# Chunk 0 in two halves with chunk 1's convolutions between, a moved weight load, and a reordered backward tail, in a speech joint-network kernel

## The chip, the core and the metric

The kernel runs on one core of a Trainium2 chip, in one launch that computes the forward pass and all gradients. The metric is the device time in microseconds (us). PE is the matmul engine, DVE the vector engine, ACT the scalar engine, POOL is GpSimd, and SP issues most of the loads.

## What is computed

```python
# x (2,16000,256), w1, w2 (3,256,256), g (2,8,256), w_f, w_g, w_o (256,256), bfloat16
h = gelu(conv(x, w1))[:, ::2]          # 3 taps, every second row kept
f = gelu(conv(h, w2))[:, ::2]          # again: (2,4000,256)
j = tanh((f @ w_f)[:, :, None] + (g @ w_g)[:, None])   # (2,4000,8,256)
out = j @ w_o
# returned: out, and by jax.vjp of grad_out (2,4000,8,256) the gradients of
# x, w1, w2, g, w_f, w_g, w_o
```

gelu is the tanh approximation; the kernel writes it as x times a sigmoid.

## The kernel before

The 4000 rows of f of each batch are cut into 8 chunks of 512 (the last has 416), 16 chunks in all. A prologue makes chunk 0's f. Then comes one stage for each chunk n. Its main line is the joint network of chunk n, two of the eight rows of g at a time (joint_units, L602): per row u, gj (L518) squares the tanh (JSQ, L523), multiplies the loaded gradient GOT by w_o (L529, into PSUM) and lets DVE make NGZ (L531); POOL sums the NGZ over u (L550); o_block (L618) makes the output (L623, evicted by ACT, L625); gwo (L664) accumulates the gradient of w_o. weave (L681) threads a second line, fill, between the units of the main line. It holds the backward pass of chunk n-1 and the convolutions of chunk n+1, in the order of the list parts (L775):

- conv_units (L227): first convolution of chunk n+1, an even and an odd half ("par"), 12 matmuls each (L246); ACT evicts (L249); the gelu follows (L197), and its derivative (L199)
- d1_units (L324, matmul L336) and d5_units (L345, matmul L366): gradient back to GF, then to GH (DVE, L369)
- gwf_units (L384, products L406) and gw2_units (L413, products L437): gradients of w_f and w_2. Their operands are first turned into rows by PE transposes (L380) and copied from PSUM (L382)
- conv2_units (L264, matmul L279), fe_units (L293, matmul L302): chunk n+1's second convolution, its gelu (FT), and FE, which the tanh (L312) reads
- e_units (L443): GH is transposed into rows in two units (L462), then per block the gradient of x (gx_block, L465, matmul L478, evicted at L481, stored at L490) and in between the gradient of w_1 (gw1, L494, matmul L500)

gelu returns its operations in two lists. The first (square, scale, sigmoid, product) is queued in later, the second (the derivative) in lazy; pump (L194) issues them a few at a time, lazy ones when later is empty. flush (L318) adds a product in PSUM to the accumulators ACC1, ACC2, ACCF.

The code's order is not yet the order on the engines: a scheduler reorders the instructions at build time, each engine then runs its own list strictly in order, and keep_in_program_order pins an instruction. All PSUM tiles but one share a ring of 7 buffers (psp, L98), taken in turn, so the eighth tile waits until the first was read. JSQ has a ring of two (jsp, L92), so the JSQ for a row u must wait for the NGZ that read the JSQ two rows earlier.

In the prologue (L692 to L760) chunk 0 goes through the same functions with its gelu split by halves of the channels (HALVES, L225), the nine blocks of the weights are transposed for the backward pass (transposed_units, L730, copied by DVE at L743), and warm (L707) issues matmuls on zeros whose result nobody reads. In the stage of chunk 0, jr_block (L597) transposes the tanh on PE; later a DMA does it. At the end (L813 on) the backward pass of chunk 15 runs alone, then the accumulators are rounded and stored, and the small gradients of g and w_g follow.

Of the kernel before, what the change touches and what calls it, by code (L numbers as in the profile page):

```python
# [22 lines left out]
P = 128  # L23
# [9 lines left out]
def kernel(  # L33
# [96 lines left out]
    def load_x(n, c):  # L130
        b, ci, c0, W = geom(n)
        t = xcp.tile([P, KT, CW + 16], BF16, name="XC")
        if c == 3 and ci > 0:
            nc.sync.dma_start_transpose(out=t[:, :, 0:W + 16], in_=xq[b, c, c0 - 16:c0 + W, :])
        else:
            if c == 3:
                nc.vector.memset(t[:, :, 0:16], 0.0)
            nc.sync.dma_start_transpose(out=t[:, :, 16:16 + W], in_=xq[b, c, c0:c0 + W, :])
        S[n]["X", c] = t
# [61 lines left out]
    def gelu(xb, W, h, gp, off, kts=((0, KT),), spare=False):  # L201
# [3 lines left out]
        first, second = [], []  # L205
        for (k0, k1) in kts:
            sq_, s_, x_ = sq[:, k0:k1, :W], s[:, k0:k1, :W], xb[:, k0:k1, :W]
            h_, gp_ = h[:, k0:k1, off:off + W], gp[:, k0:k1, off:off + W]
            first += [
                partial(nc.scalar.activation, out=sq_, in_=x_, func=ACT.Square, scale=ROOT_K),  # L210
                partial(STT, out=s_, in0=sq_, scalar=1.0, in1=x_, op0=ALU.add, op1=ALU.mult),
                partial(nc.scalar.activation, out=s_, in_=s_, func=ACT.Sigmoid, scale=GELU_A),
                partial(TT, out=h_, in0=s_, in1=x_, op=ALU.mult),
            ]
            second += [
                partial(TS, out=sq_, in0=sq_, scalar1=3.0 * GELU_A, scalar2=GELU_A, op0=ALU.mult, op1=ALU.add),
                partial(TS, out=gp_, in0=s_, scalar1=-1.0, scalar2=1.0, op0=ALU.mult, op1=ALU.add),
                partial(TT, out=sq_, in0=sq_, in1=gp_, op=ALU.mult),
                partial(TT, out=sq_, in0=sq_, in1=h_, op=ALU.mult),
                partial(TT, out=gp_, in0=sq_, in1=s_, op=ALU.add),  # L220
            ]
        return first, second


    HALVES = ((0, 1), (1, 2))  # L225

    def conv_units(n):  # L227
        b, ci, c0, W = geom(n)
        seconds = []
        st = S[n]  # L230
        HT = htp.tile([P, 2, KT, CW + 2], BF16, name="HT")
        G1 = g1p.tile([P, 2, KT, CW + 2], BF16, name="G1")
        st["HT"], st["G1"] = HT, G1
# [4 lines left out]
        taps = {0: ((1, 0, 0), (2, 1, 0), (0, 3, -1)), 1: ((0, 1, 0), (2, 3, 0), (1, 2, 0))}  # L238
        for par in range(2):
            xb = gel.tile([P, KT, CW], BF16, name="g_x")  # L240
            for mt in range(KT):
                ps = ps_f32()
                k = 0
                for (i, c, sh) in taps[par]:
                    for kt in range(KT):
                        nc.tensor.matmul(ps[:, :W], lhsT=W1[:, i, kt, mt * P:(mt + 1) * P],  # L246
                                         rhs=st["X", c][:, kt, 16 + sh:16 + sh + W], start=(k == 0), stop=(k == 5))
                        k += 1
                nc.scalar.copy(out=xb[:, mt, :W], in_=ps[:, :W])  # L249
                yield  # L250
            first, second = gelu(xb, W, HT[:, par], G1[:, par], 2, HALVES if n == 0 else ((0, KT),), n == 0)
            later.extend(first)
            seconds += second
            if n == 0:
                pump(len(first))
        lazy.extend(seconds)
        if ci > 0:
            lazy.append(lambda: nc.gpsimd.tensor_copy(out=G1[:, :, :, 1:2], in_=S[n - 1]["G1h"][:]))
        if ci < NCH - 1:
            st["G1h"] = halo.tile([P, 2, KT, 1], BF16, name="G1h")  # L260
            lazy.append(
                lambda: nc.gpsimd.tensor_copy(out=st["G1h"][:], in_=G1[:, :, :, CW + 1:CW + 2]))

    def conv2_units(n):  # L264
        b, ci, c0, W = geom(n)
        st = S[n]
        HT = st["HT"]
        if n > 0:
            pump(len(later))
        FT = ftp.tile([P, KT, CW], BF16, name="FT")  # L270
        G2 = ftp.tile([P, KT, CW], BF16, name="G2")
        st["FT"], st["G2"] = FT, G2
        xb = gel.tile([P, KT, CW], BF16, name="g_x")
        for mt in range(KT):
            ps = ps_f32()
            k = 0
            for (i, par, off) in ((1, 0, 2), (0, 1, 1), (2, 1, 2)):
                for kt in range(KT):
                    nc.tensor.matmul(ps[:, :W], lhsT=W2[:, i, kt, mt * P:(mt + 1) * P],  # L279
                                     rhs=HT[:, par, kt, off:off + W], start=(k == 0), stop=(k == 5))  # L280
                    k += 1
            nc.scalar.copy(out=xb[:, mt, :W], in_=ps[:, :W])
            yield
        first, second = gelu(xb, W, FT, G2, 0, HALVES if n == 0 else ((0, KT),), n == 0)
        if n == 0:
            for f in first:
                f()
        else:
            later.extend(first)
# [3 lines left out]
    def fe_units(n):  # L293
        b, ci, c0, W = geom(n)
        if n > 0:
            pump(len(later))
# [19 lines left out]
    first_flush = {"1": True, "2": True, "F": True}  # L316

    def flush(key, acc, ps):  # L318
        if first_flush[key]:
            nc.vector.tensor_copy(out=acc, in_=ps)  # L320
        else:
            nc.vector.tensor_tensor(out=acc, in0=acc, in1=ps, op=ALU.add)  # L322

# [60 lines left out]
    def gwf_units(n):  # L384
# [24 lines left out]
        flush("F", ACCF[:], ps[:])  # L409
        first_flush["F"] = False  # L410
        yield

    def gw2_units(n):  # L413
# [19 lines left out]
        for i, place in ((1, 0), (2, 2), (0, 4)):  # L433
# [6 lines left out]
            flush("2", ACC2[:, i, :], ps[:])  # L440
            yield
        first_flush["2"] = False
    def e_units(n):  # L443
# [50 lines left out]
        def gw1(i):  # L494
# [10 lines left out]
            flush("1", ACC1[:, i, :], ps[:])  # L505

        for k, (o, M) in enumerate(bl):
# [4 lines left out]
        first_flush["1"] = False  # L512
# [184 lines left out]
    nc.gpsimd.dma_start(out=WG[:], in_=w_g.rearrange("(kt p) n -> p kt n", p=P))  # L697
    nc.sync.dma_start(out=W2[:], in_=w2.rearrange("i (kt p) n -> p i kt n", p=P))
    nc.sync.dma_start(out=WF[:], in_=w_f.rearrange("(kt p) n -> p kt n", p=P))
    nc.sync.dma_start(out=WO[:], in_=w_o.rearrange("(kt p) n -> p kt n", p=P))  # L700
    idle = xcp.tile([P, KT, CW + 16], BF16, name="XC")
    nc.vector.memset(idle[:], 0.0)
# [51 lines left out]
    for c in (1, 0, 3, 2):  # L754
        load_x(1, c)
    for _ in chain(warm(16), small_units(), conv_units(0), transposed_units(), warm(4), conv2_units(0), warm(16), fe_units(0)):
        pass
# [4 lines left out]
    for n in range(G):  # L762
        back, fwd = n > 0, n + 1 < G
        conv = conv_units(n + 1) if fwd else iter(())
        parts = []
        if back:
            for (o, M) in blocks(window(n - 1)[1] - window(n - 1)[0]):
# [7 lines left out]
                      islice(d5, 1), islice(gw2, 1), d5, islice(gw2, nhg - 2), gwf, gw2]  # L775
        else:
            parts += [conv, iter([None] * 3)]
        if fwd:
            parts.append(conv2_units(n + 1))
        if back:  # L780
            parts.append(islice(e, 6))
        else:
            parts.append(iter([None] * 3))
# [6 lines left out]
        for up in range(U // 2):  # L790
# [17 lines left out]
            if up == U // 2 - 1:  # L808
# [3 lines left out]
                lazy_on[0] = False  # L812
    n = G - 1  # L813
# [3 lines left out]
    for _ in chain(d1_units(n), d5_units(n), gwf_units(n), gw2_units(n), e_units(n)):  # L817
        pass


    for i in range(KK):
        t_ = gel3.tile([P, 512], BF16, name="g_sq", tag="g_sq")
        nc.scalar.copy(out=t_[:], in_=ACC1[:, i, :])
        nc.sync.dma_start(out=out_2[i].rearrange("(dt p) n -> p dt n", p=P), in_=t_[:].rearrange("p (k n) -> p k n", k=KT))
        t_ = gel3.tile([P, 512], BF16, name="g_s", tag="g_s")
        nc.vector.tensor_copy(out=t_[:], in_=ACC2[:, i, :])
        nc.sync.dma_start(out=out_3[i].rearrange("(dt p) n -> p dt n", p=P), in_=t_[:].rearrange("p (k n) -> p k n", k=KT))
    t_ = gel.tile([P, 512], BF16, name="g_x", tag="g_x")
    nc.vector.tensor_scalar(out=t_[:], in0=ACCF[:], scalar1=-1.0, scalar2=None, op0=ALU.mult)
    nc.sync.dma_start(out=out_5.rearrange("(dt p) n -> p dt n", p=P), in_=t_[:].rearrange("p (k n) -> p k n", k=KT))  # L830
    t_ = gel.tile([P, 512], BF16, name="g_x", tag="g_x")
    nc.scalar.copy(out=t_[:], in_=GWO_ps[:].rearrange("p k v -> p (k v)"))
    nc.sync.dma_start(out=out_7.rearrange("(dt p) n -> p dt n", p=P), in_=t_[:].rearrange("p (k n) -> p k n", k=KT))

    NGGE = const.tile([P, B, KT, U], FP32, name="NGGE")
    nc.vector.tensor_reduce(out=NGGE[:].rearrange("p b k u -> p (b k u)"),
                            in_=NGGEc[:].rearrange("p b k u c -> p (b k u) c"),
                            axis=mybir.AxisListType.X, op=ALU.add)
    NGGEb = const.tile([P, B, KT, U], BF16, name="NGGEb")
    nc.vector.tensor_copy(out=NGGEb[:], in_=NGGE[:])  # L840
    GWG_ps = ps_f32()
    for b in range(B):
        gg = ps_f32()
        for kt in range(KT):
            nc.tensor.matmul(gg[:U, 0:D], lhsT=NGGEb[:, b, kt, :], rhs=WGT[:, kt, :], start=(kt == 0), stop=(kt == KT - 1))
        gg_sb = gxp.tile([U, D], BF16, name="gg_sb")
        nc.scalar.activation(out=gg_sb[:], in_=gg[:U, 0:D], func=ACT.Copy, scale=-1.0)
# [43 lines left out]
```

## Time and profile before

| what | us |
|---|---|
| median of 3 runs | 867.71 (865.87 to 876.6) |
| the profiled execution: time | 865.23 |
| its span, first to last instruction | 863.5 |
| PE busy | 830.8 (96%) |
| ACT busy | 685.7 (79%) |
| DVE busy | 603.8 (70%) |
| POOL busy | 410.6 (48%) |
| longest chain: share of PE, DVE, ACT | 51%, 30%, 13% |

The span is 1.73 us shorter than the time of the same execution. In the profile's lines a time is a start within the span, the number after it the duration, and square brackets give the idle time before an instruction and what ended it. Instructions of an engine overlap a little: a DVE operation shown with 0.68 us lets the next one start after 0.61.

### The profile page before, as it was taken

What the parts mean: (1) busy time and instruction counts of PE and PEld (TensorE: products, weight loads), DVE (VectorE), ACT (ScalarE), POOL (GpSimd) and SP (SyncE); (2) the same over time, 40 slices, a digit from 0 to 9 for tenths busy, and PEclk for the clock granted to TensorE, in tenths of its full rate; (3) what the DMA queues carried; (4) which work ended last, traced back from release to release, by engine and by line L of the source; (5) the groups of instructions that cost most, each with busy time, mean ns of one, the idle gap of its engine ahead of it and who ended that gap; (6) DMA issues with size and microseconds to landing.
All of it is one profiled execution on the core that took longest, in us unless ns stands there. A gap on an engine that the chain in (4) does not pass through costs nothing.

```text
span 863.5 us, 17775 instructions
## 1 busy us (share of the span) xinstructions
PE 830.8 (96%) x6648; PEld 598.9 (69%) x6648; DVE 603.8 (70%) x1194; ACT 685.7 (79%) x1067; POOL 410.6 (48%) x457
## 2 busy tenths in 40 slices
PE   8878999999999999999999999999999999999997
PEld 4455776767777677777766677776766867777875
DVE  4797949669495784949578495875949579495553
ACT  4889896986969869696996969788696986969534
POOL 1264553544544544555454455453554544455651
PEclk9999999999999999999999999999999999999999
DMA  9998999999999999999899999999999999999942
GB/s 187 211 215 195 189 250 224 224 243 193 258 206 227 226 217 233 212 227 219 211 203 214 234 215 240 227 210 250 177 263 236 205 211 219 219 243 219 215 140 91
DMA packets 382455, 185.66 MB, mean 215 GB/s; under 512 B 330160, under 2 KB 366280, under 8 KB 382368
## 3 DMA queue, kind: packets, MB, share of 16 engines
q1 hardware_dynamic: 362400, 114.35, 76.4%
q0 software_dynamic: 19968, 70.18, 27.9%
q8 instruction: 52, 0.85, 0.4%
q14 instruction: 35, 0.29, 0.1%
HBM read 54.43 MB, written 50.34 MB: 121 GB/s over the span
## 4 chain that ended last, share of the span: by engine, by line
PE 51%; DVE 30%; ACT 13%; issue 3%; DMA 2%; POOL 0%; ACTq 0%; POOLq 0%; DVEq 0%
PE ps L500 7%; PE ps L246 7%; PE GWO_ps L672 7%; PE ps L529 7%; PE ps L478 7%; PE ps L623 6%; DVE NGZ L531 6%; DVE G L199 5%; DVE g_sq L199 5%; DVE g_s L197 5%; DVE GH L369 3%; ACT JSQ L523 3%; ACT JT L312 3%; PE pst L380 3%; PE ps L366 3%
## 5 line engine op out<-in xcount | busy, mean ns | idle before, releaser
L550 POOL TENSOR_TENSOR ACCN<-ACCN,NGZ 128x1024 f32<-128x1024 f32 (+1 forms) x80 | 170.4, 2130 | 126.5 <-DVE NGZ L531 124.0
L531 DVE SCALAR_TENSOR_TENSOR NGZ<-JSQ,ps 128x512 bf16<-128x512 bf16 (+1 forms) x256 | 163.4, 669 | 83.5 <-ACT GX L481 47.7
L523 ACT ACTIVATE JSQ<-JT 128x1024 bf16<-128x1024 bf16 (+1 forms) x128 | 135.3, 1060 | 86.6 <-DVE NGZ L531 86.6
L312 ACT ACTIVATE JT<-FE,GE 128x512 bf16<-128x512 f32 (+1 forms) x256 | 171.0, 736 | 0.1
L625 ACT CAST OUT<-ps 128x512 bf16<-128x512 f32 x248 | 147.7, 614 | 3.8 <-PE ps L623 3.3
L623 PE MATMUL ps<-WO,JT 128*128 128x256 bf16 x992 | 148.1, 272 | 0.9 <-DVE NGZ L531 0.5
L529 PE MATMUL ps<-GOT,WOT 128*128 128x512 bf16 (+1 forms) x512 | 138.4, 374 | 1.7 <-DVE JR L382 1.1
L672 PE MATMUL GWO_ps<-GO,JR 128*128 128x256 bf16 x992 | 139.7, 273 | 0.0
L197 DVE SCALAR_TENSOR_TENSOR g_s<-g_sq,g_x 128x1024 bf16<-128x1024 bf16 (+1 forms) x45 | 74.6, 1657 | 57.1 <-ACT g_sq L197 57.1
L623 PEld LDWEIGHTS <-JT 128*128 128x128 bf16 x992 | 94.4, 98 | 24.9 <-issue 1.4
L672 PEld LDWEIGHTS <-JR 128*128 128x128 bf16 x992 | 95.1, 98 | 18.2 <-issue 1.1
L322 DVE TENSOR_TENSOR ACC<-ACC,ps 128x512 f32<-128x512 f32 x90 | 59.4, 682 | 66.6 <-PE ps L500 62.0
L478 PE MATMUL ps<-W1T,GH 128*128 128x256 bf16 (+2 forms) x768 | 104.2, 273 | 0.0
L500 PE MATMUL ps<-rows,X 128*128 128x256 bf16 (+2 forms) x768 | 94.2, 272 | 8.2 <-DVE rows L382 8.2
L246 PE MATMUL ps<-XC,W 128*128 128x512 bf16 (+1 forms) x384 | 91.1, 374 | 2.5 <-DMA XC<-in_x_dram 2.1
L500 PEld LDWEIGHTS <-X 128*128 128x128 bf16 (+2 forms) x768 | 74.5, 98 | 23.1 <-issue 11.5
L652 POOL DMA_DIRECT2D out_dram<-OUT x64 | 49.6, 775 | 85.2 <-ACT OUT L625 82.8
L481 ACT CAST GX<-ps 128x512 bf16<-128x512 f32 (+2 forms) x128 | 74.4, 592 | 15.0 <-PE ps L478 7.8
L478 PEld LDWEIGHTS <-GH 128*128 128x128 bf16 (+2 forms) x768 | 75.0, 99 | 15.6 <-issue 1.7
L529 PEld LDWEIGHTS <-WOT 128*128 128x128 bf16 x512 | 49.1, 98 | 43.9 <-issue 2.6
L490 POOL DMA_DIRECT2D out_dram<-GX x64 | 35.9, 560 | 87.3 <-ACT GX L481 81.0
L382 ACT COPY rows<-pst 128x1024 bf16<-128x1024 bf16 x64 | 63.0, 1018 | 9.6 <-PE pst L380 9.5
(139 smaller groups left out, 1264.5 us busy)
## 6 DMA issues: line engine op xcount, KB each, us to landing
GO<-in_grad_out_dram SPq DMA_DIRECT2D x56, 512.0 KB, 5.3
out_dram<-OUT POOLq DMA_DIRECT2D x56, 512.0 KB, 5.6
X<-in_x_dram POOLq DMA_DIRECT2D x58, 320.0 KB, 8.0
out_dram<-GX POOLq DMA_DIRECT2D x58, 256.0 KB, 4.1
JR<-JT SPq DMA_TRANSPOSE x240, 5.1
GO<-in_grad_out_dram SPq DMA_DIRECT2D x8, 384.0 KB, 4.1
out_dram<-OUT POOLq DMA_DIRECT2D x8, 384.0 KB, 4.7
GOT<-in_grad_out_dram SPq DMA_TRANSPOSE x128, 4.6
```

Of the source, the lines that this page charges most:

```text
L197: later.popleft()()
L246: nc.tensor.matmul(ps[:, :W], lhsT=W1[:, i, kt, mt * P:(mt + 1) * P], rhs=st["X", c][:, kt, 16 + sh:16 + sh + W], start=(k == 0), stop=(k ...
L312: nc.scalar.activation(out=JT[:, mt, :W], in_=S[n]["FE"][:, mt, :W], func=ACT.Tanh, bias=GE[:, b, mt, u:u + 1], scale=1.0)
L478: nc.tensor.matmul(ps[:Mx, cj * D:(cj + 1) * D], lhsT=GH[:, par, kt, j:j + Mx], rhs=W1T[:, i, kt, :], start=(k == 0), stop=(k == last))
L500: nc.tensor.matmul(ps[:, dt * D:(dt + 1) * D], lhsT=st["X5", o][:M, i + 2 * par, dt * P:(dt + 1) * P], rhs=t[:M, j + 2 * par:j + 2 * par + ...
L523: nc.scalar.activation(out=JSQ[:, :, :W], in_=JT[:, :, :W], func=ACT.Square)
L529: nc.tensor.matmul(ps[:, :W], lhsT=WOT[:, kt, mt * P:(mt + 1) * P], rhs=GOT[:, kt, :W], start=(kt == 0), stop=(kt == KT - 1))
L531: nc.vector.scalar_tensor_tensor(out=NGZ[:, mt, :W], in0=JSQ[:, mt, :W], scalar=1.0, in1=ps[:, :W], op0=ALU.subtract, op1=ALU.mult, accum_ ...
L550: nc.gpsimd.tensor_tensor(out=out, in0=in0, in1=st["NGZ", u][:, :, :W], op=ALU.add)
L623: nc.tensor.matmul(ps[:M, j * V:(j + 1) * V], lhsT=st["JT", u][:, kt, o:o + M], rhs=WO[:, kt, :], start=(kt == 0), stop=(kt == KT - 1))
L625: nc.scalar.copy(out=OUT[:M, k, :], in_=ps[:M, :])
L672: nc.tensor.matmul(GWO_ps[:, dt, :], lhsT=JR[:M, k, j, dt, :], rhs=GO[:M, k, j * V:(j + 1) * V], start=(n_gwo[0] == 0), stop=(n_gwo[0] == ...
```

## The change

- Chunk 0: its first and second convolution are cut into column halves (CUTS), each product 256 wide. Its square is made by DVE (a product and a scaling) and not by ACT. Its derivative goes into lazy through behind, which pins its first operation.
- Chunk 1's convolutions run in the prologue, between the two halves of chunk 0's second convolution and before FE; eight of the nine weight transposes move into the stage of chunk 0. warm(16) before FE goes.
- Chunk 1's x is loaded ahead of w_f and of the GOT and GO loads; two of its four tiles lie in OUT's buffers. w_o is loaded by POOL's queue. The zeros for warm are half a GOT buffer.
- In every stage e_units' two transposing units move up between the units of gw2.
- In the last backward pass gw1 and the blocks of gx alternate in another order (block 0 last), flush rounds and stores the sums itself, and the small gradients are made between d1 and e.

```diff
+        if n == 1 and c > 1:
+            t = outp.tile([P, 4, 2 * V], BF16, name="OUT")...
...
+            if spare:
+                square = [partial(TT, out=sq_, in0=x_, in1=x_, op=ALU.mult),
+                          partial(TS, out=sq_, in0=sq_, scalar1=GELU_K, scalar2=None, op0=ALU.mult)]
+            else:
+                square = [partial(nc.scalar.activation, out=sq_, in_=x_, func=ACT.Square, scale=ROOT_K)]
...
+    CUTS = ((0, CW // 2), (CW // 2, CW))
...
+    def behind(ops):
+        lazy.append(lambda: tc.keep_in_program_order(ops[0]()))
+        lazy.extend(ops[1:])
+    def first_conv_units():
...
+        for half, (a, e) in enumerate(CUTS):
+            for par in range(2):
+                for mt in range(KT):
+                    conv_product(0, par, mt, xs[par], a, e)
+                    yield
+                for f in parts[par][0][half]:
+                    f()
+        for par in range(2):
+            behind(parts[par][1])
...
+    def flush(n, key, i, ps):
+        if n == G - 1:
+            t = gel3.tile([P, 512], BF16, name="g_sq", tag="g_sq")
...
+                nc.vector.tensor_tensor(out=t[:], in0=acc, in1=ps, op=ALU.add)
+            store_small(out, t)
...
+        if n == G - 1:
+            for i in range(KK):
+                gw1(i)
+                yield from gx_block(*bl[-1 - i])
+            yield from gx_block(*bl[0])
+            return
...
+    nc.gpsimd.dma_start(out=WO[:], in_=w_o.rearrange("(kt p) n -> p kt n", p=P))
     nc.sync.dma_start(out=W2[:], in_=w2.rearrange("i (kt p) n -> p i kt n", p=P))
+    for c in (1, 0, 3, 2):
+        load_x(1, c)
     nc.sync.dma_start(out=WF[:], in_=w_f.rearrange("(kt p) n -> p kt n", p=P))
-    nc.sync.dma_start(out=WO[:], in_=w_o.rearrange("(kt p) n -> p kt n", p=P))
...
-    for _ in chain(warm(16), small_units(), conv_units(0), transposed_units(), warm(4), conv2_units(0), warm(16), fe_units(0)):
+    for _ in chain(warm(16), small_units(), first_conv_units(), warm(4), islice(conv2, 2),
+                   islice(conv, 2), conv2, islice(transposed, 1), conv, first_fe_units()):
...
-                      islice(d5, 1), islice(gw2, 1), d5, islice(gw2, nhg - 2), gwf, gw2]
+                      islice(d5, 1), islice(gw2, 1), d5, islice(gw2, nhg - 2), gwf, islice(e, 1), islice(gw2, 1),
+                      islice(e, 1), gw2]
         else:
-            parts += [conv, iter([None] * 3)]
+            parts.append(transposed)
...
-            parts.append(islice(e, 6))
+            parts.append(islice(e, 4))
...
-    for _ in chain(d1_units(n), d5_units(n), gwf_units(n), gw2_units(n), e_units(n)):
+    for _ in chain(d1_units(n), islice(small, 1), d5_units(n), islice(small, 1), gwf_units(n), islice(small, 1),
+                   gw2_units(n), small, e_units(n)):
```

The built program of the changed kernel gives the order on the engines. In the stage of chunk 2, from the products of w_f on, these are the lists before and after (PE, then ACT from the second JSQ of the pair on):

```
PE before: w2 products, w2 products x2, NGZ products x2, conv2, NGZ, conv2, NGZ, GH transposes, out, GH transposes, out, gx
PE after:  GH transposes, w2 products, GH transposes, NGZ x2, w2 products, NGZ, w2 products, NGZ, conv2, out, conv2, out, gx
DVE before: ACCF, G1 x2, ACC2 x3, NGZ x4, GH rows, g_s, GH rows
DVE after:  ACCF, G1 x2, GH rows, ACC2, GH rows, NGZ x2, ACC2, NGZ, ACC2, NGZ, g_s
ACT before: JSQ, g_x, g_x, g_sq, OUT, JSQ, OUT, g_s, GX, GX
ACT after:  JSQ, JSQ, g_x, OUT, g_x, OUT, g_sq, GX, GX, g_s
```

(g_x is the eviction of conv2's product, g_sq its square, g_s first DVE's scaling and then ACT's sigmoid; GWO products and the evictions between are left out.) Nine of the fourteen stages that make a next chunk have this ACT order; in the other five one g_x stands between the two JSQ, and in three of these an OUT too.

## The prediction

> **What bounds the kernel now.** I read the page first (busy shares, groups), then the windows stage by stage, then the waits, then the timeline of one steady stage on each engine, and the chain of waits for the end. The page says that PE is busy nearly always, and which of its waits is large:
>
> ```profile
> PE 830.8 (96%) x6648; PEld 598.9 (69%) x6648; DVE 603.8 (70%) x1194; ACT 685.7 (79%) x1067; POOL 410.6 (48%) x457
> L500 PE MATMUL ps<-rows,X 128*128 128x256 bf16 (+2 forms) x768 | 94.2, 272 | 8.2 <-DVE rows L382 8.2
> ```
>
> The windows show three different regimes. In a steady stage (52.4 us) PE is idle for 1.2 us. From 12 to 75 us DVE is the full engine: 55.2 of 62.5 us busy, while PE's 51.5 includes 4.6 of matmuls on zeros:
>
> ```profile
> 128.40:180.80 52.40, 51.22 (x410) 37.17 (x409) 36.95 (x70) 43.03 (x67) 25.15 (x27) 1.00 1.11 232
> 12.19:27.80 15.61, 14.46 (x92) 7.45 (x91) 15.14 (x44) 10.85 (x20) 0.19 (x1) 1.00 1.07 213
> 27.80:74.68 46.88, 37.08 (x269) 23.33 (x268) 40.10 (x87) 40.90 (x63) 25.96 (x20) 1.00 0.93 199
> ```
>
> (stretch, its length, PE, PEld, DVE, ACT, POOL busy, clock, DMA share, GB/s). Inside a steady stage, in PE's, DVE's, ACT's and POOL's timelines:
>
> ```profile
> 143.86 1.21 PE L437 MATMUL ps<-rows 128*128 128x256 bf16 x8
> 145.34 1.91 PE L437 MATMUL ps<-rows 128*128 128x256 bf16 x16
> 157.68 1.03 PE L500 MATMUL ps<-rows,X 128*128 128x256 bf16 x8 [0.83 <-DVE rows L382]
> 160.51 1.03 PE L302 MATMUL ps<-FT,WF 128*128 128x512 bf16 x4
> ```
> ```profile
> 146.58 0.67 DVE L322 TENSOR_TENSOR ACCF<-ACCF,ps 128x512 f32<-128x512 f32 x1
> 147.17 1.28 DVE L199 TENSOR_TENSOR G<-g_sq,g_s 128x1024 bf16<-128x1024 bf16 x2
> 148.38 1.87 DVE L322 TENSOR_TENSOR ACC<-ACC,ps 128x512 f32<-128x512 f32 x3
> 150.78 0.68 DVE L531 SCALAR_TENSOR_TENSOR NGZ<-JSQ,ps 128x512 bf16<-128x512 bf16 x1
> 154.70 2.33 DVE L197 SCALAR_TENSOR_TENSOR g_s<-g_sq,g_x 128x1024 bf16<-128x1024 bf16 x1 [1.41 <-ACT g_sq L197]
> 156.95 0.68 DVE L382 COPY rows<-pst 128x1024 bf16<-128x1024 bf16 x1
> 158.15 0.69 DVE L197 TENSOR_TENSOR FT<-g_s,g_x 128x1024 bf16<-128x1024 bf16 x1 [0.19 <-ACT g_s L197]
> ```
> ```profile
> 151.56 1.06 ACT L523 ACTIVATE JSQ<-JT 128x1024 bf16<-128x1024 bf16 x1 [5.96 <-DVE NGZ L531]
> 152.52 1.06 ACT L282 CAST g_x<-ps 128x512 bf16<-128x512 f32 x2
> 153.61 1.06 ACT L197 ACTIVATE g_sq<-g_x 128x1024 bf16<-128x1024 bf16 x1
> ```
> ```profile
> 151.61 4.33 POOL L550 TENSOR_TENSOR ACCN<-ACCN,NGZ 128x1024 f32<-128x1024 f32 x2 [2.91 <-DVE NGZ L531]
> ```
>
> The reader is to see that DVE is behind PE here: it evicts the products of w_2 at 148.38, three microseconds after the first was made. g_s starts under POOL's second sum, takes 2.33 instead of 1.22 (129.25 in the same timeline), and the second row copy stands behind it; PE waits. FT is done at 158.84, 1.7 us before PE wants it at 160.51. JSQ waits for NGZ (151.46 to 151.56).
>
> **Part 1, GH's rows.** I lay the new lists on this stage, with start to start times of the same rows (NGZ, ACC and a row copy 0.61, OUT and g_x about 0.5, JSQ 0.96, eight products 0.87, two NGZ products 0.43, six conv2 matmuls 1.30, transposes 0.44, out 0.44).
>
> PE from 143.86: GH transposes, GWO, w2 products to 145.60, transposes, NGZ products to 146.91. The second w2 product takes the ring's buffer of the w_f product, which DVE leaves at 147.25: wait 0.39. The third takes that of the first GH transposes. Its copy is now on DVE at 148.38, behind the derivative, and ends at 149.06: PE arrives at 148.60, waits 0.51. Then w2 149.98, NGZ 150.41, conv2, out, conv2, out to 153.87, and 2.62 more to L500 at 156.49. That no longer waits and ends at 158.24, against 158.55 before. So the two waits that go (1.0 between the halves of L500, 0.18 at the first w2 product) are mostly paid back in PSUM waits: **0.31 gained**. PE wants FT at 158.24 + 1.96 = 160.20.
>
> What is queued behind: on DVE nine operations from 148.38 put the last NGZ of the pair at 153.23, done 153.92 (before 152.67). In nine stages ACT's second JSQ waits for exactly that NGZ, and g_x, OUT, g_x, OUT and g_sq now stand behind it: JSQ 154.0, then 0.96 + 0.5 + 0.48 + 0.47 + 0.46, g_sq at 156.88, g_s on DVE 1.09 later at 157.97, 1.23 + 0.04 to ACT's sigmoid at 159.24, 1.09 to FT's product, 0.69 + 0.05 to PE: 161.07. (POOL's second sum, 154.0 to 156.1, no longer meets g_s; that is in it.) PE waits 0.87 where it did not wait, and FE comes **0.56 later** than before. 9 x 0.56 = +5.0.
>
> In the three stages with a g_x and an OUT between the JSQs, g_sq comes 1.0 earlier, FT about 160.05: no wait, -0.31 each. In the two of chunk 7 and 15, 0.5 earlier, about 0. Part 1: **+4.1**. Bounds: all 1.18 gained in 14 stages, -16.5 (no row excludes a DVE that is earlier); the measured waits on L500 are 8.2, so I hold -11 for the real end. Upwards, a further whole sum of POOL (2.12) before the last NGZ, 9 x 2.1 = +19 on top. I take the middle, since every step of it has a row of this stage.
>
> **Part 2, the front.** PE would gain most: 4.6 us on zeros from 18.35 on, 3.0 in the wait for FT, 2.1 for x. But DVE sets this stretch. It gains six squares (0.34 + 0.20 start to start, from the 128x512 rows): +3.2. The derivative in whole operations, not halves, saves 8.5 - 7.4 = 1.1. So 55.2 + 2.1 = 57.3 us of work up to GF (L338). It starts at 11.3, when the first two 128x256 evictions (0.37, L586's row) are done, not 12.2. Idle of DVE: following the new list until the first NGZ I get 1.15 behind chunk 1's square on ACT, 0.46 before FT's first half, 0.95 before the first JR, and about 1 in small gaps; the 1.64 behind JSQ at 73.45 stays. 5.2 us. The derivative now lies in 35 to 61 us beside POOL's sums; before, the stretched operations lost 6.7 us there in all (56.28 took 2.56, not 0.68). Setting each sum against what DVE has behind it I get 1.4 more. 11.3 + 57.3 + 5.2 + 1.4 = 75.2, against 74.68: **+0.5**. Bounds: no idle after 27 us and no more contention, 71.2 (-3.5); seven sums that each hold DVE for their whole 2.13, 14.9 - 6.7, +8. I take the accounting. ACT (5.6 us of chunk 1's work moved before the first tanh, which starts at 27.75 for 27.00) and PE are not full there.
>
> w_o behind w_g on POOL's queue (issue 0.75, landing 5.3 as w_g's) is there at about 10, needed at 21: 0. Four transposes ahead of GOT on SP (1.3 to 1.5 each) bring the first GOT from 13.7 to about 20, needed near 27; x of chunk 1 lands at 15 to 18.5, needed at 16.9 and 21: 0, at most 0.5. POOL's memset and SP's fewer issue wait for nobody.
>
> The Trainium skill (TensorE: Matmul & The Clock Gate, What's actually happening) says that an idle window of about 3.4 us halves PE's clock, which speaks against dropping warm(16). PE stood 2.97 us before FT (60 to 63) at a granted clock of 1.00; the new longest gap is 1.6 (28.9 to 30.5), so by that rule too nothing changes.
>
> The skill (SBUF - State Buffer, SBUF: two separate sides) calls the port that DVE shares with GpSimd an exclusive lock, taken by DVE operations with two SBUF inputs. The stretched rows agree; by it alone the front would come to its upper bound.
>
> **Part 3, the end.** Before, after the last gx (856.66): 2.36 of small gradients, 0.60 ACT, SP's store with 1.8 to landing, 861.5. Now those matmuls lie earlier and shift ACT's row copies by 0.6 (they stand before and among the w_f rows). After the GH transposes PE no longer has a gx (1.42) while DVE copies the rows, and waits about 1.35. Last gx 858.5, ACT 0.59, 0.3 to POOL's issue, a 256 KB store, 2.6 to landing: 862.1. **+0.6** (bounds -1.4 with both shifts hidden, +2.1 with the landing of 4.1 of the page's median).
>
> **Sum.** Against the profiled execution (863.5 span + 1.73 around it = 865.23): +4.1 + 0.5 + 0.6 = +5.2, **870.4 us**. The median of the runs shown lies 2.5 above that execution, their lowest 0.6; 2% (17 us) is about what a measurement can tell from no change, so this is no change.
>
> **The rivals.** (a) The FT wait doesn't come, the PSUM waits do: 14 x -0.31 + 1.1 = -3.2, 862.0. For it: g_x between other operations could slip ahead if NGZ ends before 153.0. (b) The wait goes and nothing replaces it, because DVE's derivative ends before PE needs the ring: -11 + 1.1, 855.3. Against it: DVE is packed from 140 to 153. (c) Slower by over 2%: POOL's first sum (from 151.6) also holds an ACC2 or NGZ, so that the last NGZ ends 2.1 later: 9 x 2.7 - 0.9 + 1.1, about 890. It decides from an NGZ end of 155.2 on (1.9 a stage). Against it: NGZ at 151.99 ran under the sum in 0.68. (d) The front is PE's after all and gives its 4.6 + 3.0 + 2.1: 870.4 - 10.2, 860. (e) The front at its upper bound of contention: 878. (f) A PE gap over 3 us in the prologue halves the clock for some matmuls, as after 861 us, where it is 0.50: +3, 873.
>
> **How the numbers follow.** Chances: the forecast 0.50 (its own range 866 to 876), a 0.17, b 0.14, d 0.06, e 0.05, c 0.04, f 0.04. 855 to 878 leaves out c and about half of b and e with what lies beyond, under 0.2. Faster by over 2% needs all of b and d (0.02), slower c (0.04).
>
> **What would show it.** Right: L500 has no wait on rows in steady stages, a new wait of L359 for FT of about 0.9 in nine of them, waits of the w2 products (L504) for DVE, a stage of about 52.95; DVE about as full up to 75 us; first L404 near 74. Wrong: L359 without a wait, the stage under 52.1; or the first L404 before 71.

## The result and the profile after

The changed kernel takes 877.42 us (median of 8 runs, 876.57 to 880.35) and the kernel before 867.84 in the runs beside it: a ratio of 1.0101, 95% interval 1.0070 to 1.0132. That is 9.6 us more, where 870.4 was forecast, and it lies inside the range of 855 to 878, near its upper end, and outside the 866 to 876 that the forecast itself was given. The profiled execution took 877.04 with a span of 875.2 (before 865.23 and 863.5).

The page's shares, and the group that had the large wait:

```profile
PE 828.8 (95%) x6598; PEld 604.1 (69%) x6672; DVE 585.1 (67%) x1187; ACT 680.1 (78%) x1064; POOL 409.0 (47%) x458
L567 PE MATMUL ps<-rows,X 128*128 128x256 bf16 (+2 forms) x768 | 92.3, 273 | 0.9 <-DVE rows L450 0.9
```

L567 is the old L500. Its wait for the copied rows fell from 8.2 to 0.9, and yet the span is 11.7 longer. The view of waits names what came in its place (total, times, longest). Before, PE waited for FT once, in the front:

```profile
PE ps L302 <- DVE FT L197: 3.0, 1, 3.0
```
```profile
PE ps L359 <- DVE FT L201: 6.0, 9, 0.7
PE ps L504 <- DVE rows L450: 3.1, 9, 0.3
PE ps L504 <- DVE ACCF L387: 2.3, 10, 0.3
```

Windows, as before: length, PE, PEld, DVE, ACT, POOL, clock, DMA share, GB/s. The first is one steady stage, the next two are the front, from the first work of DVE to the first tanh, and from there to GF (L406):

```profile
138.07:190.98 52.91, 50.92 (x405) 37.18 (x409) 35.65 (x70) 42.79 (x67) 25.02 (x26) 1.00 1.10 228
13.31:31.12 17.81, 15.94 (x101) 10.52 (x102) 14.75 (x34) 12.92 (x25) 0.59 (x1) 0.91 1.02 213
31.12:78.77 47.65, 37.02 (x276) 24.41 (x279) 42.72 (x93) 37.31 (x57) 23.57 (x20) 0.93 0.80 169
```

The stage grew from 52.40 to 52.91. The clock column, 1.00 in all three windows before, is below 1 in the front.

I cut the span at the first product of the loss gradient with w_f (d1, L404, before L336), since it opens the backward work of each chunk. First d1: 73.78 before, 77.87 after, so the front lost 4.1. From first to last d1: 759.29 before, 765.21 after, 5.9 lost in the stages. From the last d1 to the end of the span: 30.4 before, 32.1 after, 1.7 lost at the end. Together 11.7, the whole difference of the spans.

### The profile page after: what moved, and what is told of

Read it like the earlier page. It is cut to its first block, busy times and chain, and to the rows that moved or that the text cites. A ratio compares the mean times of both kernels' runs of the same rounds, so it can differ in the third digit from the quotient of the medians.

```text
span 875.2 us, 17760 instructions
## 1 busy us (share of the span) xinstructions
PE 828.8 (95%) x6598; PEld 604.1 (69%) x6672; DVE 585.1 (67%) x1187; ACT 680.1 (78%) x1064; POOL 409.0 (47%) x458
## 4 chain that ended last, share of the span: by engine, by line
ACT 34%; DVE 29%; PE 22%; issue 10%; DMA 2%; POOL 1%; SPq 0%; ACTq 0%; POOLq 0%; DVEq 0%
ACT JT L369 10%; DVE NGZ L603 7%; DVE G L203 5%; ACT OUT L697 5%; DVE g_sq L203 4%; ACT JSQ L595 4%; ACT g_sq L201 4%; ACT GX L548 4%; DVE GH L437 3%; DVE g_s L201 3%; PE ps L695 3%; PE GWO_ps L744 3%; PE ps L545 2%; ACT g_x L245 2%; PE ps L567 2%
## 5 line engine op out<-in xcount | busy, mean ns | idle before, releaser
L601 PE MATMUL ps<-GOT,WOT 128*128 128x512 bf16 (+1 forms) x470 | 134.1, 373 | 6.0 <-DVE JR L450 2.4
L695 PEld LDWEIGHTS <-JT 128*128 128x128 bf16 x992 | 96.3, 98 | 33.6 <-issue 3.7
L201 DVE SCALAR_TENSOR_TENSOR g_s<-g_sq,g_x 128x1024 bf16<-128x1024 bf16 (+1 forms) x45 | 56.8, 1263 | 93.2 <-ACT g_sq L201 93.1
L567 PE MATMUL ps<-rows,X 128*128 128x256 bf16 (+2 forms) x768 | 92.3, 273 | 0.9 <-DVE rows L450 0.9
L242 PE MATMUL ps<-XC,W 128*128 128x512 bf16 (+2 forms) x383 | 88.8, 371 | 0.9 <-DMA XC<-in_x_dram 0.9
L387 DVE TENSOR_TENSOR ACC<-ACC,ps 128x512 f32<-128x512 f32 x84 | 57.3, 682 | 47.0 <-PE ps L567 46.9
L567 PEld LDWEIGHTS <-X 128*128 128x128 bf16 (+2 forms) x768 | 74.5, 98 | 14.1 <-issue 2.4
L242 PEld LDWEIGHTS <-W 128*128 128x128 bf16 x408 | 41.1, 101 | 37.7 <-issue 1.1
```

The lines of the kernel that those rows point to most:

```text
L201: later.popleft()()
L242: nc.tensor.matmul(ps[:, :e - a], lhsT=W1[:, i, kt, mt * P:(mt + 1) * P], rhs=S[n]["X", c][:, kt, 16 + sh + a:16 + sh + e], start=(k == 0) ...
L567: nc.tensor.matmul(ps[:, dt * D:(dt + 1) * D], lhsT=st["X5", o][:M, i + 2 * par, dt * P:(dt + 1) * P], rhs=t[:M, j + 2 * par:j + 2 * par + ...
L601: nc.tensor.matmul(ps[:, :W], lhsT=WOT[:, kt, mt * P:(mt + 1) * P], rhs=GOT[:, kt, :W], start=(kt == 0), stop=(kt == KT - 1))
L695: nc.tensor.matmul(ps[:M, j * V:(j + 1) * V], lhsT=st["JT", u][:, kt, o:o + M], rhs=WO[:, kt, :], start=(kt == 0), stop=(kt == KT - 1))
```

## Experiments

A theory for each of the three pieces. Stages: the moved rows make the pair's last NGZ later, ACT's second JSQ waits for it and holds g_x; the rival was that another edit lengthens the stage. Front: three suspects, namely w_o's transfer, the lower clock, and the pin on chunk 0's derivative; the rival was that DVE has the same sum to do whatever their order. End: its new order.

A caution on the ratios: in the first two sets the runs of the kernel before spread widely, so that intervals are wide, and there the cuts of the traces carry the verdicts. The last set is narrow.

**GH's rows alone** (the kernel before, and only this):

```
-                      ... gwf, gw2]
+                      ... gwf, islice(e, 1), islice(gw2, 1), islice(e, 1), gw2]
-            parts.append(islice(e, 6))
+            parts.append(islice(e, 4))
```

> The kernel before with GH's rows moved up alone (front and end as before). Main theory: the stage goes from 52.39 to about 52.91 as in the changed kernel, because ACT's second JSQ waits for the pair's last NGZ and holds g_x and g_sq, so FT comes late; over the stages +5 to +6, so a span of 868.5 to 869.5 and a ratio near 1.006. Rival: the rows' move costs nothing and the longer stage comes with the other edits; then the span is within 1 of 863.5 and no FE product waits for FT. First d1 near 73.8 by both.

Measured: 873.09, ratio 1.0038 (1.0003 to 1.0073), span 873.4. The waits of the w_2 products (here L437) are those of the changed kernel to the digit, and of the eleven waits for FT one (3.0, in the front) was there before:

```profile
PE ps L302 <- DVE FT L197: 9.7, 11, 3.0
PE ps L437 <- DVE rows L382: 3.1, 9, 0.3
PE ps L437 <- DVE ACCF L322: 2.3, 10, 0.3
```

Steady stages take 52.88 to 52.90, and first to last d1 766.24, 6.95 over before (of which 1.3 lie in one stage, from 703 on, and are not in the changed kernel). The longer stage comes from the rows alone; the rival falls. The miss: its first d1 came at 76.76, though its front is that of the kernel before. There the clock was 0.65 from 9 to 12 and 0.81 from 31 to 40. So the front before is not 73.78 in every execution. Its operations are those of the kernel before, so the two can be laid side by side. DVE's first work comes 1.43 later (13.62 for 12.19), behind a wait of PE for g (0.75) and a first stretch at half clock. The clock is again half from 33.76 to 37.18, while PE makes chunk 1's convolution, and the gelu behind it comes 3.0 later, here before and then with the rows alone:

```profile
38.62 1.22 DVE L197 SCALAR_TENSOR_TENSOR g_s<-g_sq,g_x 128x1024 bf16<-128x1024 bf16 x1 [2.75 <-ACT g_sq L197]
```
```profile
41.61 1.23 DVE L197 SCALAR_TENSOR_TENSOR g_s<-g_sq,g_x 128x1024 bf16<-128x1024 bf16 x1 [4.32 <-ACT g_sq L197]
```

The first d1 is late by the same 3.0. In the run of the ring of five in the kernel before (below), which has this front and one stretch at half clock, from 30.81 to 37.64, the first d1 comes at 77.08, 3.3 late. So in this front, where DVE waits for that convolution, half clock there goes with a loss of 1.6 to 3.3.

**w_o back on SP, behind w_f:**

```
-    nc.gpsimd.dma_start(out=WO[:], ...)
     nc.sync.dma_start(out=WF[:], ...)
+    nc.sync.dma_start(out=WO[:], ...)
```

> The changed kernel with w_o loaded by SP behind w_f, as before. Theory A (w_o's 128 KB on POOL's queue delay x of chunk 0 and w_g): XC has landed when conv of chunk 0 asks for it (no wait of 0.88 at 10.1), conv's granted clock stays near 1.00 instead of 0.50 between 9.6 and 16, first d1 about 2 to 3 earlier than 77.87. Theory B (x of chunk 1 and w_2, issued earlier by SP, are what competes, or PE's idle alone lowers the clock): XC still lands near 11, clock 0.50 until about 16, first d1 within 1 of 77.87. w_o itself lands later; if the first transposes of w_o then wait, that is seen on L816.

Measured: 875.92, ratio 1.0091 (1.0052 to 1.0130). Conv began at 9.57 and ran through without a wait for XC, at a clock of 1.00; DVE's first work came at 11.48 for 13.31, the second d1 at 127.22 for 129.33. Theory A, here and in every other profile: with w_o on POOL's queue PE waits for w_g 0.8 to 1.5 (six profiles) and for XC 0.2 to 0.9 (the five of them without added zeros); with w_o on SP (five profiles) it waits 0.4 for w_g and never for XC. How much that is worth varies: PE also waits for g (GR), up to 1.5 and up to 2.2, and DVE's first work comes at 11.8 to 14.5 with w_o on POOL's queue, at 10.9 to 12.1 on SP's.

**More zeros:** `warm(16)` becomes `warm(20)`, and a `warm(4)` stands ahead of the first convolutions.

> The changed kernel with 20 instead of 16 matmuls on zeros at the start and 4 more between the small products and the convolutions of chunk 0. Theory A (the clock falls because PE was idle for about half of 6.8 to 11): clock 1.00 through the convolutions, which end near 17 instead of 18.6; DVE's pause of 1.08 at 14.8 goes; first d1 1 to 2.5 earlier than 77.87. Theory B (DVE's list sets the front from 13.3 on whatever the clock does): clock 1.00, first d1 within 0.7 of 77.87. Theory C (the clock falls for another reason than idleness): 0.50 again between 9.6 and 16.

Measured: 877.45, ratio 1.0101 (1.0011 to 1.0192). The clock did stay up in the first stretch, and fell in the second as before:

```profile
9.00:16.00 7.00, 6.32 (x60) 5.28 (x61) 3.36 (x10) 2.65 (x7) 0.00 (x0) 1.00 1.17 223
47.00:54.00 7.00, 4.88 (x26) 3.48 (x26) 6.04 (x14) 4.00 (x7) 3.35 (x2) 0.56 0.58 148
```

First d1 77.40 for 77.87, second 128.85 for 129.33: 0.5. Theory B. In this pair of executions, the first drop of the clock, which looks worst in the trace, costs half a microsecond: DVE has a full list behind it. Only the front of this profile is read, since in its stages the clock fell twice more, at 454 and at 570, and its span is 884.4.

**No pin on chunk 0's derivative:**

```
-        lazy.append(lambda: tc.keep_in_program_order(ops[0]()))
-        lazy.extend(ops[1:])
+        lazy.extend(ops)
```

> The changed kernel without the pin on the derivative of chunk 0 (its operations are queued as those of other chunks, so the scheduler may put them earlier). Theory A: pinned, they stand on DVE from 38 to 51 ahead of the second pair's NGZ, PE waits for the ring from 44 to 50 and its clock is 0.50 from 47 to 54; without the pin NGZ comes 2 to 4 earlier, clock stays 1.00 there, DVE's pause of 2.57 at 60 shrinks and the first d1 is 2 to 3 earlier than 77.87. Theory B: DVE has the same sum to do either way, and the first d1 is within 1 of 77.87.

Measured: 874.19, ratio 1.0053 (1.0013 to 1.0094). First d1 72.30 for 77.87, second 125.43 for 129.33, span 872.4. DVE's part of the front, first work to the last chunk-0 NGZ, in the changed kernel and then without the pin:

```profile
13.31:78.77 65.46, 52.97 (x375) 34.93 (x380) 57.47 (x126) 50.23 (x82) 24.15 (x21) 0.92 0.86 181
```
```profile
13.10:73.20 60.10, 50.33 (x375) 33.69 (x380) 54.98 (x126) 49.46 (x82) 31.41 (x21) 0.97 0.97 197
```

DVE does 126 operations in both; they take 2.5 less without the pin, and the idle time falls from 8.0 to 5.1. Why is seen on DVE, pinned:

```profile
38.38 2.28 DVE L203 TENSOR_TENSOR rows<-rows,G 128x1024 bf16<-128x1024 bf16 x1
...
45.59 0.67 DVE L603 SCALAR_TENSOR_TENSOR NGZ<-JSQ,ps 128x512 bf16<-128x512 bf16 x1
...
48.01 2.00 DVE L203 TENSOR_TENSOR rows<-rows,FT 128x1024 bf16<-128x1024 bf16 x1
49.94 0.67 DVE L603 SCALAR_TENSOR_TENSOR NGZ<-JSQ,ps 128x512 bf16<-128x512 bf16 x1
...
62.81 1.23 DVE L201 SCALAR_TENSOR_TENSOR g_s<-g_sq,g_x 128x1024 bf16<-128x1024 bf16 x1 [2.57 <-ACT g_sq L201]
```

and what PE did beside it:

```profile
46.32 0.38 PE L448 MATMUL pst<-ident,JT 128*128 128x128 bf16 x4 [1.76 <-DVE NGZ L603]
...
50.67 1.95 PE L695 MATMUL ps<-WO,JT 128*128 128x256 bf16 x8 [1.95 <-DVE NGZ L603]
```

Without the pin DVE takes the same four NGZ one behind the other from 42.94 on, and has them done by 45.4 (pinned: 50.6):

```profile
42.94 0.69 DVE L603 SCALAR_TENSOR_TENSOR NGZ<-JSQ,ps 128x512 bf16<-128x512 bf16 x1
...
57.37 1.23 DVE L201 SCALAR_TENSOR_TENSOR g_s<-g_sq,g_x 128x1024 bf16<-128x1024 bf16 x1 [2.79 <-ACT g_sq L201]
```

Pinned, the derivative stands in DVE's queue ahead of the second pair's NGZ, two of its products meet POOL's sums (2.28 and 2.00 for 0.68), PE has no PSUM buffer and stops, its clock halves, and conv2 of chunk 1 comes late. Unpinned the derivative is done before 36, in part in gaps that DVE has there when it is pinned.

Two points of theory A did not come. DVE's pause for conv2 did not shrink: it is 2.57 with the pin and 2.79 without, so that pause is not what the pin costs. What shrinks is the work (2.5) and the idle time outside that pause (5.4 to 2.3). And the clock did stay at 1.00 from 47 to 54, but fell elsewhere, from 30.86 to 34.28, after PE had waited for FT:

```profile
31.47 1.01 PE L318 MATMUL ps<-FT,WF 128*128 128x256 bf16 x4 [4.92 <-DVE FT L307]
```

Still the first d1 comes 5.6 earlier, more than the 2 to 3 that were expected; theory B, the same sum in any order, falls. Whether DVE's longer list or PE's stop sets the later time is not separated: up to the pause both are about 5.5 late. Of the 5.6 gained at the first d1, 3.9 are left at the second and 2.9 at the last.

**The end as before** (last gx and w_1's products in the old order, sums evicted behind them, small gradients last):

> The changed kernel with the end as before: stores of the sums after the last gx, gx and the products of w_1 in their old order, small gradients last. Theory: the end (from the first d1 of the last chunk to the last landing, 32.1 in the changed kernel, 30.4 before) goes back to about 30.4, so the time is 1.7 under the changed kernel's. Rival: the end is longer only because the stage ahead of it leaves work behind; then it stays near 32.

Measured: 876.67, ratio 1.0100 (1.0034 to 1.0167); the last d1 at 843.92, span 874.3, so an end of 30.38. Theory: the new end costs 1.7. The median does not show it: four runs, and the first d1 of this execution at 79.27, which is 1.4 later than in the changed kernel.

**NGZ written over JSQ**, one ring of five tiles for two rings of two and three:

```
-    jsp = pool("jsp", 2)
-    ngzp = pool("ngzp", 3)
+    jsp = pool("jsp", 5)
...
-        NGZ = ngzp.tile([P, KT, CW], BF16, name="NGZ")
+        NGZ = JSQ
```

> The changed kernel with NGZ written over JSQ in one ring of five tiles, in place of a ring of two for JSQ and one of three for NGZ (same memory). ACT's JSQ then waits for a POOL sum five tiles back and no longer for the last NGZ of the pair. Theory: FE's products no longer wait for FT (6.0 us in 9 stages in the changed kernel) and the stage falls from 52.91 to 52.1 to 52.4, 5 to 9 us in all. Rival 1: g_x is held by something else next in line (a conv2 product, PSUM), FT stays late and the stage stays within 0.15 of 52.91. Rival 2: JSQ's new wait for POOL's sums is longer than the old one and the stage grows over 53.

> The kernel before with the same ring of five in place of two and three. Theory: before, PE does not wait for FT; an earlier g_sq moves g_s out from under POOL's second sum (it took 2.33 for 1.22), so the second copy of GH's rows comes earlier and the wait of L500 (0.83 a stage) shrinks: stage 51.9 to 52.4. Rival: nothing that PE waits for moves, 52.39 stays.

Measured in the changed kernel: 875.67, ratio 1.0074 (1.0045 to 1.0103). No steady FE product waits for FT any more; ACT takes g_x at 153.29 as soon as PE has made it:

```profile
153.29 0.59 ACT L254 CAST g_x<-ps 128x512 bf16<-128x512 f32 x1 [6.27 <-PE ps L251]
```

So the JSQ ring is what held g_x. But the stage is 52.63, only 0.28 less. PE now waits for PSUM:

```profile
PE ps L694 <- DVE JSQ L602: 8.1, 14, 1.9
PE ps L433 <- DVE GH L436: 7.1, 8, 0.9
```

In the kernel before the same ring brings the stage from 52.39 to 52.04, but the short chunk and the one behind it lose 1.5 and 0.6, and the time is 866.65, ratio 1.0000 (0.9953 to 1.0048). With this ring in both, the moved rows cost 0.59 a stage, as much as without it. So the late FT is where the cost shows, but taking that wait away does not bring the time back. My reading, which no run separates, is that DVE evicts PSUM no sooner, and with FT in time PE waits for a PSUM buffer. FT came in time, as the theory has it; the stage lies between its 52.1 to 52.4 and rival 1.

**No pin and w_o on SP together:**

> The changed kernel without the pin and with w_o on SP behind w_f. Theory: both act on the front; the second d1 (of chunk 1), 129.33 in the changed kernel, 125.43 without the pin, 127.22 with w_o on SP, comes at 124 to 125.5. Rival: they save the same time, DVE's list being full either way, and the second d1 stays at 125.4 or later.

Measured: 872.40, ratio 1.0027 (0.9991 to 1.0063). First d1 71.30, second 124.45: the two savings add, mostly (4.9 of 3.9 + 2.1).

**The front alone**, with GH's rows and the end as before, in four forms: as changed; without pin and with w_o on SP; that with 20 + 4 zeros; that with the ring of five.

> The changed kernel's front alone, with the pin and w_o on POOL: GH's rows and the end as before. Theory: the changed kernel's 877.4 less 5.9 for the stages and 1.7 for the end, 869 to 871, ratio about 1.003; second d1 near 129.3, stage 52.39. Rival: the front costs nothing in the median (its late second d1 belongs to single executions, before has such ones too), 867 to 868.

> The same without the pin and with w_o on SP behind w_f. Theory: 872.4 as measured with the moved rows and the new end, less 5.9 and 1.7, 864 to 866; second d1 near 124.5, stage 52.39; faster than before by 2 to 3. Rival: the time saved in the front is lost in the first stages behind it, 867 to 868.

> The same as the kernel without pin and with w_o on SP, with 20 instead of 16 zero matmuls at the start and 4 more ahead of the convolutions of chunk 0. Theory: the granted clock stays 1.00 from 9 to 16, the convolutions end 1 to 2 earlier, 0.5 to 1.5 less in all. Rival: DVE sets the front and the clock there costs nothing: the same time within 0.5, or 0.5 more for the later convolutions.

> The same as the kernel without pin and with w_o on SP, with NGZ written over JSQ in a ring of five. Theory: the stage falls to 52.04 in eight full stages as in the kernel before with this ring (2.8 less), while the short chunk and the one behind it lose what they lost there (1.5 and 0.6): 863 to 865, no more than 1 under the kernel without it. Rival: the loss at the short chunk came by chance, then 862 to 863.

| front alone | median us | ratio, 95% interval | first d1 | second d1 |
|---|---|---|---|---|
| as changed | 869.42 | 1.0033 (1.0021 to 1.0046) | 79.34 | 130.75 |
| no pin, w_o on SP | 863.18 | 0.9960 (0.9948 to 0.9971) | 69.64 | 122.75 |
| and more zeros | 863.82 | 0.9986 (0.9953 to 1.0018) | 70.92 | 124.01 |
| and ring of five | 861.79 | 0.9963 (0.9931 to 0.9995) | 70.22 | 122.17 |

(Before in this set: 866.85.) The front as changed costs 2.6 in the median. Without the pin and with w_o on SP the same front is faster than before, by 3.7, and beats both kernels: what is left of the front's change gains time, and two of its side conditions took that away. Which part of it gains (the split of chunk 0, chunk 1's convolutions between, the squares on DVE, fewer zeros) was not run alone. The extra zeros bring nothing that can be seen. The ring of five has the lowest median, but two of its six runs lie at 866.5 and 870.3, and its interval holds that of the kernel without it: inconclusive.

Not run alone: x of chunk 1 behind the first loads of grad_out, as before.

## Why the prediction was right or wrong

**Part 1, the stage: mechanism and size right, the count wrong.** Forecast 52.95, measured 52.91. In one stage, PE, ACT and DVE of the changed kernel:

```profile
151.33 1.03 PE L504 MATMUL ps<-rows 128*128 128x256 bf16 x8 [0.20 <-DVE ACCF L387]
153.14 1.03 PE L504 MATMUL ps<-rows 128*128 128x256 bf16 x8 [0.34 <-DVE rows L450]
165.07 1.02 PE L359 MATMUL ps<-FT,WF 128*128 128x512 bf16 x3 [0.66 <-DVE FT L201]
```
```profile
158.00 1.06 ACT L595 ACTIVATE JSQ<-JT 128x1024 bf16<-128x1024 bf16 x1 [1.36 <-DVE NGZ L603]
158.96 0.57 ACT L255 CAST g_x<-ps 128x512 bf16<-128x512 f32 x1
159.43 0.59 ACT L697 CAST OUT<-ps 128x512 bf16<-128x512 f32 x1
159.91 0.60 ACT L255 CAST g_x<-ps 128x512 bf16<-128x512 f32 x1
160.38 0.61 ACT L697 CAST OUT<-ps 128x512 bf16<-128x512 f32 x1
160.86 1.09 ACT L201 ACTIVATE g_sq<-g_x 128x1024 bf16<-128x1024 bf16 x1
```
```profile
157.22 0.68 DVE L603 SCALAR_TENSOR_TENSOR NGZ<-JSQ,ps 128x512 bf16<-128x512 bf16 x1
161.98 1.23 DVE L201 SCALAR_TENSOR_TENSOR g_s<-g_sq,g_x 128x1024 bf16<-128x1024 bf16 x1 [4.08 <-ACT g_sq L201]
```

The order on ACT is the one that was laid out: JSQ behind the last NGZ, then g_x, OUT, g_x, OUT, g_sq. The three waits are 0.20, 0.34 and 0.66, forecast 0.39, 0.51 and 0.87, and the difference is one of counting: the forecast went from start to start (0.87 for eight products), the profile counts from the end that it shows (1.03). By starts the second product of w_2 comes 3.43 behind the first transposes of GH, at 147.90 (143.86 in the forecast; there 3.44), the third 5.24 (5.25), FE's 17.17 (17.21). g_s takes 1.23 again, clear of POOL's sum, as said. The step that failed is "in the three stages with a g_x and an OUT between the JSQs ... no wait, -0.31 each": of these three the first got 0.10 shorter, and the stage of the short chunk and the one behind it 0.15 and 0.23 longer. In those two PE had not waited for rows before, so there was no such wait to gain: the 0.31 of the laid-out stage was taken for every stage. Of the nine, seven got 0.51 to 0.57 longer and the two around chunk 9 0.83 and 0.88; the two forecast at "about 0" each got 0.11 longer. The sum is +5.9 for +4.1. And what the ring of five showed belongs here: the path was laid out rightly, but it is not the only thing that holds the stage, since with that ring, without a late FT, the moved rows still cost 0.59.

**Part 2, the front: wrong by its three terms.** +0.5 was forecast. The trace gives +4.1, but against an execution whose front was early: with the front of before, the second d1 lay at 125.34, at 128.52 (rows alone) and at 127.65 (ring of five) in three profiles. By medians the front costs 2.6. The steps that failed: "w_o behind w_g on POOL's queue ... 0" and x "0, at most 0.5": w_o's 128 KB travel with the last x and w_g, and DVE starts at 13.31, not at 11.3 (11.48 with w_o on SP). Idle time of DVE "5.2" was 8.0: I followed the list only "until the first NGZ". The pauses that I named, 1.15, 0.46, 0.95 and 1.64, came as 1.14, 0.36, 0.26 and 1.51; missing are 1.08 at 15.87, while the convolution ran at half clock, and 2.57 at 62.81, for conv2 of chunk 1. The work, 57.3 and 1.4 of contention, was 57.5 in all. The three come to +2.0, +2.8 and -1.2, so 78.77 for 75.2.

Rival (f), the clock, came true without the gap of over 3 us that I had made its condition. Its price is not one number: the zeros put the first drop in the changed front at 0.5, what the second costs no run separates, and in the front of before half clock over chunk 1's convolution goes with 1.6 to 3.3, where the rival has +3. So the execution that I forecast from was an early one, in which no drop came; that was luck, and it makes the front look worse in the cuts than by medians.

I had weighed the Trainium skill (TensorE: Matmul & The Clock Gate, What's actually happening) by the longest gap, 1.6, against its idle window of about 3.4. No single wait of PE in the front was longer than 1.95, and the clock halved twice. The same section of the Trainium skill says that the window runs freely. What the trace shows is that the share within a window counts (below).

On the exclusive lock of the Trainium skill (SBUF - State Buffer, SBUF: two separate sides): the products at 38.38 and 48.01 lie on POOL's sums and take 2.0 to 2.3, as it would have it. The upper bound of +8 was not reached.

**Part 3, the end:** +0.6 forecast, +1.7 measured. The wait for the rows was 0.92 for 1.35, and the last gx ended 25.75 behind the last d1, which is 858.8 on the old scale for 858.5. The last store landed 2.3 behind its issue at 869.75 (before, 1.8 behind 859.67); counted from the last d1 that is 0.5 later than before, forecast +0.6. So the sum was right up to the landing, and what failed is its last step, that the span ends with the landing of the last store. The trace shows another path. A DRAIN on POOL's queue begins with the issue of POOL's last store, before and after:

```profile
857.95 0.56 POOL L490 DMA_DIRECT2D out_dram<-GX  x1 [0.49 <-ACT gg_sb L847]
L886 POOLq DRAIN  x3: 46/103/4743, 857.9 to 863.2; - x3
```
```profile
869.75 0.54 POOL L557 DMA_DIRECT2D out_dram<-GX  x1 [0.76 <-ACT GX L548]
L955 POOLq DRAIN  x3: 46/103/4722, 869.7 to 875.0; - x3
```

(In the DRAIN rows: shortest, median and longest in ns, first and last start.) The longest takes 4.74 and 4.72, ends 2.4 after the last store has landed in the changed kernel, and the span ends 0.8 behind it. POOL issues its last store 24.88 behind the last d1 before and 26.67 after: 1.8 later, which is all that the end lost, within rounding. Before, SP made the last store and POOL's came earlier; the new order puts a block of gx last, and POOL stores it. A last store on SP was not run.

**Sum.** With the front by medians, and the stages and the end by the cuts, 2.6 + 5.9 + 1.7 = 10.2; measured 9.6. The forecast was right in sign and in its largest term, and short by the front, by the count of the stages and by the path at the end. Of the 7.0 between the forecast and the median, 2.6 lie in the execution that it started from, 865.23 for a median of 867.84.

## What to carry to other kernels

Before an operation is pinned or moved up in an engine's queue, list what stands behind it and who waits for that, which gaps of the engine it gives up, and what it then runs beside, in the prologue as in the steady loop. A gain counted in one stage holds only for the stages that have the wait. A wait that disappears on the bounding engine can come back at the next resource if the engine that frees buffers has no less to do. For the end of a kernel, look at what the last instruction waits for: here it is a queue, and not the last landing. A small load on an idle queue is not free while the loads that everything waits for are still under way.

## What was not expected of the hardware

The granted clock of TensorE changes on a grid: in all 14 traces the stretches at half clock last 3.41, 6.83 or 10.24 us, multiples of 3.41 (cut off only by the span's end), and where the grid lies differs from one execution to the next. It goes with how busy PE was in the grid's window just before. In the changed kernel:

```profile
6.29:9.70 3.41, 2.03 (x20) 1.15 (x19) 0.62 (x4) 0.00 (x0) 0.00 (x0) 1.00 1.28 167
9.70:13.11 3.41, 2.53 (x14) 1.59 (x12) 0.03 (x1) 0.58 (x2) 0.00 (x0) 0.50 1.19 266
43.83:47.25 3.42, 1.22 (x14) 0.79 (x12) 3.42 (x9) 2.91 (x6) 0.66 (x3) 1.00 1.19 185
47.25:50.66 3.41, 0.65 (x6) 0.42 (x4) 3.41 (x7) 2.00 (x3) 2.22 (x1) 0.50 0.97 192
```

A window with 2.03 of 3.41 busy (60%) was followed by half clock, and so was one with 1.22 (36%). Over all traces every window at full clock with a PE share under 0.41 was followed by half clock, none over 0.60, and between them it went either way. So several short waits can halve the clock, as the single one of 4.92 without the pin did, and the same front can lose it in one execution and keep it in another.

The end of the span hangs on POOL's queue: in all 14 traces the DRAIN that begins with POOL's last store takes 4.72 to 4.74, ends 2.4 to 2.8 after that store has landed, and the span ends 5.48 to 5.51 behind the issue of that store, also in the kernel before, where a store of SP was issued and landed later.
